# A fused spectral transform and two MLPs in float32 on one core: where GpSimd's background work and six low parts are issued

## The chip, the core and the metric

The kernel runs on one core of a Trainium2 chip. Five engines work side by side: TensorE multiplies matrices (PE in the profile, its weight loads PEld), VectorE (DVE) and ScalarE (ACT) read and write both on-chip memories, GpSimd (POOL) reads and writes SBUF only, and SyncE (SP) issues the DMA transfers. Each engine works through its own instructions strictly in order and waits on semaphores. The metric is the device time of one execution in microseconds (us), as the median of several runs.

## What is computed

The input x is 2 x 3008 x 256 numbers. The reference takes a discrete Fourier transform along both axes, keeps the real part, and sends each of the 6016 tokens through two MLPs of 256 -> 2048 -> 256:

```python
def _attn_ref(x):
    X = np.fft.fft(x, axis=1)
    X = np.fft.fft(X, axis=2)
    return X.real.astype(np.float32)

def _moe_ref(x, w_in, w_out):
    h = x @ w_in
    r = np.maximum(h, 0.0)
    g = r * r
    return (g @ w_out).astype(np.float32)

def _moe2_ref(x, w_in, w_out):
    h = x @ w_in
    g = h * (1.0 / (1.0 + np.exp(-1.702 * h)))
    return (g @ w_out).astype(np.float32)
```

## The kernel before

Every float32 factor is held as a high part (rounded to fp32r) and a low part (the rest), and each product is three matmuls: high by high, high by low, low by high. "Low part" below always means the subtraction that makes such a rest.

The kernel has two halves. The first half transforms x and runs the first MLP; it is a loop of 128 steps, and in the profiled execution it lasts until about 480 us. The second half is the second MLP, in an order written out by hand; the change does not touch it.

A step of the first half takes one block of up to 378 frequency pairs (eight blocks, `blocks`) and one group f of 128 of the 2048 hidden features. Step i consists of:

- `front1` (L462 to L464): six matmuls into one of two `psa` tiles of PSUM. The first three fill its first bank, the other three its second bank.
- VectorE, L805, L807, L808: p from the first bank, then the two halves of h as p plus and minus the second bank. Only after L808 is the `psa` tile free for the front of two `psa` tiles later.
- ScalarE, L814, L815, L817: ReLU, square, and the high part `gh`. In the 14 steps of `SV`, VectorE does ReLU and square in one instruction (L812).
- `low_part` (recorded on L78 as gl<-h,gh): gl = h - gh. It is called for step i in iteration i + 1, behind that iteration's L805 to L808. GpSimd does it, except for the steps in `VSTEPS`, where VectorE does. Only when it has been done is the h buffer free.
- `back` (L477): twelve matmuls of the step four earlier (`LAG`), from its gh and gl, into the block's two accumulators in `psb`.

The h buffers are four (tiles of the tag h, `bufs=4`). Two of them are lent to y from time to time: a block's hidden features are visited in several turns (`turns`), and when a turn ends that isn't the block's first, the partial sums of y that lie in DRAM are fetched into two tiles of the same tag three steps earlier (`ahead`, L589), VectorE adds the accumulators to them (`store`, L602) and SyncE writes them back (L605). This happens in iterations 27, 39, 43 and 51. While the two tiles are lent out, the steps take turns on the other two h buffers: by the addresses of the program, h of step 26 takes the buffer of step 24, h of 27 that of 25, h of 28 that of 26; and from step 38 to 45 h of step k takes that of step k - 2. The accumulators `psb` are both taken by one turn, so the first `back` of the next turn waits for the two additions; it is held back by one step (`held`).

Beside the steps runs background work (`background(i)`, from `PLAN`): widening of weights (`conv` in steps 3 to 36, `w2a` from 58, `w2b` from 88), and the transform of the second batch (`fold3` from step 31, `fold4` from 38, `fold5` from 45, then `even10` and so on). Its instructions go to all engines. GpSimd's share of it from step 18 on is small: the first subtraction of each `fold` (L281), one addition (L207) and some low parts of weights (L78, w and w2i), four sums for each of two weight groups (L234), one low part of eo in each of a few places, and copies of one column (L341, L342).

The code is not issued as traced: a scheduler orders each engine's instructions by when it expects them to be ready, in the order of tracing among those that are ready. From step `THROTTLE` = 18 on, background instructions of VectorE and of ScalarE may not be put ahead of the step's L808 (`last_v`) and L817 (`last_a`); `tc.issue_after(ins)` does that. It fixes the order on that one engine and adds no semaphore wait. GpSimd's background instructions have no such bound.

Steps are counted from 0; the k-th L805 in order of time belongs to step k, and so do the k-th L814 and L817 where no step of `SV` or of the start has been left out. All lines are those of the kernel before.

Of the kernel before, what the change touches and what calls it, by code (L numbers as in the profile page):

```python
# [13 lines left out]
ALU = mybir.AluOpType  # L14
# [27 lines left out]
THROTTLE = 18  # L42

LOW = {(0, 0, 0): "V", (0, 0, 1): "V", (0, 0, 2): "G", (0, 0, 3): "V", (0, 1, 0): "G", (0, 1, 1): "G", (0, 1, 2): "G", (0, 1, 3): "V", (1, 0, 0): "G", (1, 0, 1): "G", (1, 0, 2): "G", (1, 0, 3): "G", (1, 1, 0): "G", (1, 1, 1): "G", (1, 1, 2): "V", (1, 1, 3): "V"}
VSTEPS = {44, 45, 50, 69, 71, 79, 82, 99, 101, 109}
RA = {(0, 0, 0), (0, 0, 1), (0, 0, 2), (0, 0, 3), (0, 1, 1), (0, 1, 2), (0, 1, 3), (1, 0, 1),
      (1, 0, 2), (1, 1, 2), (1, 0, 3), (1, 1, 3)}
EOG = {1, 2, 3}
# [17 lines left out]
def spectral_two_mlps_kernel(  # L66
# [5 lines left out]
    V, A, G, T = nc.vector, nc.scalar, nc.gpsimd, nc.tensor  # L72

    def f32(ap):
        return ap.bitcast(F32)

    def sub(eng, o, a, b):
        eng.tensor_tensor(out=o, in0=a, in1=f32(b), op=ALU.subtract)  # L78
# [19 lines left out]
    def ps_b():  # L98
        return psb.tile([P, 2, 512], F32, tag="b", name="psb")
# [29 lines left out]
    def load_w(mlp, kind, g, slot=None):  # L129
        seen.append((mlp, kind, g))  # L130
        r = raw_tile((len(seen) - 1) % 2 if slot is None else slot)
        nc.sync.dma_start(r, ((w1i, w1o), (w2i, w2o))[mlp][kind][g].bitcast(U32))
        raws[mlp, kind, g] = r
# [134 lines left out]
    def keep_busy(o, k):  # L268

        for _ in range(k):  # L270
            last = T.matmul(o, lhsT=still, rhs=still, start=True, stop=True, skip_group_check=True)
        return last
# [178 lines left out]
    def front1(j, f):  # L451
        wd = WID[blocks[j][1]]
        w = weights[0, 0, f // 4]
        c0 = (f % 4) * P
        t = eo[blocks[j]]
        pq = ps_a()
        if at_step[0] == 0 and j == 0:
            keep_busy(pq[:, 0, 384:512], WARM["first"])
        for par in range(2):
            o = pq[:, par, 0:wd]  # L460
            fs = slice(par * 512 + c0, par * 512 + c0 + P)
            T.matmul(o, lhsT=w[:, 0, fs], rhs=t[:, par, 0, 0:wd], start=True, stop=False)  # L462
            T.matmul(o, lhsT=w[:, 0, fs], rhs=t[:, par, 1, 0:wd], start=False, stop=False)  # L463
            T.matmul(o, lhsT=w[:, 1, fs], rhs=t[:, par, 0, 0:wd], start=False, stop=True)  # L464
        return pq

    def back(j, f, first, last, ecs=range(2)):
        wd = WID[blocks[j][1]]
        if first:
            acc[j] = [ps_b(), ps_b()]  # L470
        gh, gl = gst[j, f]
        w = weights[0, 1, f // 4]
        for ec in ecs:
            e0 = (f % 4) * 256 + ec * P
            for hl, gi in ((0, 0), (0, 1), (1, 0)):
                for s in range(2):
                    T.matmul(  # L477
                        acc[j][ec][:, s, 0:wd],
                        lhsT=w[:, hl, e0:e0 + P],
                        rhs=(gh, gl)[gi][:, s, 0:wd],  # L480
                        start=(first and hl == 0 and gi == 0),
                        stop=(last and hl == 1),
                    )


    def run(gen, n=1 << 30):
        for _ in range(n):
            item = next(gen, None)
            if item is None:
                return False  # L490
            item()
        return True
# [74 lines left out]
    def background(i):  # L567
        for name, rate, job in plan.pop(i, ()):
            live.append((name, rate, job()))
        for entry in list(live):  # L570
            if not run(entry[2], int((i + 1) * entry[1]) - int(i * entry[1])):
                live.remove(entry)
                gone.add(entry[0])
        for name in due.get(i + 1, ()):
            for entry in list(live):
                if entry[0] == name:
                    run(entry[2])
                    live.remove(entry)
                    gone.add(name)
            assert name in gone, name  # L580
# [3 lines left out]
    def ahead(j):  # L584

        wd = WID[blocks[j][1]]
        leaving[j] = [m.tile([P, 2, NP], F32, tag="h", name="o", bufs=4) for _ in range(2)]
        for ec, o in enumerate(leaving[j]):
            nc.sync.dma_start(o[:, :, 0:wd], ydram[j][:, ec, :, 0:wd])  # L589
# [14 lines left out]
                (A.copy, V.tensor_copy)[ec](o, ap)  # L604
            nc.sync.dma_start(y[:, ec, :, 0:wd], o)  # L605

    pend = None
    n = len(steps)


# [162 lines left out]
    for i in range(n):  # L773

        if i == PLAN["fold5"][2]:
            xp.release()
            cv2 = tc.alloc_tile_pool(name="cv2", bufs=1, side="left", reuse_waits="tile")
            w2a = tc.alloc_tile_pool(name="w2a", bufs=3, side="left", reuse_waits="tile")
            load_w(1, *order[0])
            load_w(1, *order[1])  # L780
        if i == PLAN["odd1"][2]:
            cp.release()
            zp.release()
            w2b = tc.alloc_tile_pool(name="w2b", bufs=3, side="left", reuse_waits="tile")
        at_step[0] = i
        if LAG <= i + 1 < n and steps[i + 1 - LAG][4] and steps[i + 1 - LAG][1] in ydram:
            ahead(steps[i + 1 - LAG][1])
        j, f = steps[i][1:3]
        ps = front1(j, f)
        if i == 1:  # L790
            o = ps_b()[:, 0, 0:128]
            for _ in range(WARM["second"]):
                tc.keep_in_program_order(keep_busy(o, 1))
        done = steps[i - LAG][1:] if i >= LAG else None
        if held:
            back(*held.pop())
        if done and done[2] and i > LAG and i < n - 1:
            held.append(done)
        elif done:
            back(*done)  # L800
        wd = WID[blocks[j][1]]
        h = m.tile([P, 2, NP], F32, tag="h", name="h", bufs=4)
        hv = h[:, :, 0:wd]
        p = m.tile([P, NP], F32, tag="p", name="p")
        V.scalar_tensor_tensor(out=p[:, 0:wd], in0=e128[blocks[j]][:, 0:wd], scalar=w1n_t[:, 0, f:f + 1],  # L805
                               in1=ps[:, 0, 0:wd], op0=ALU.mult, op1=ALU.add)
        V.tensor_tensor(out=h[:, 0, 0:wd], in0=p[:, 0:wd], in1=ps[:, 1, 0:wd], op=ALU.add)  # L807
        last_v = V.tensor_tensor(out=h[:, 1, 0:wd], in0=p[:, 0:wd], in1=ps[:, 1, 0:wd], op=ALU.subtract)  # L808
        if done and done[3]:
            store(*done[:2])  # L810
        if i in SV:
            V.scalar_tensor_tensor(out=hv, in0=hv, scalar=0.0, in1=hv, op0=ALU.max, op1=ALU.mult)  # L812
        else:
            A.activation(out=hv, in_=hv, func=AF.Relu)  # L814
            A.activation(out=hv, in_=hv, func=AF.Square)  # L815
        gh = mg.tile([P, 2, NP], F32R, tag="gh", name="gh", bufs=5)
        last_a = A.copy(gh[:, :, 0:wd], hv)  # L817

        def low_part(i, key, h, gh):
            pw = WID[blocks[key[0]][1]]  # L820
            gl = mg.tile([P, 2, NP], F32R, tag="gl", name="gl", bufs=5)
            sub(G if i not in VSTEPS else V, gl[:, :, 0:pw], h[:, :, 0:pw], gh[:, :, 0:pw])
            gst[key] = (gh, gl)

        if pend:
            low_part(*pend)
        pend = (i, (j, f), h, gh)
        with ExitStack() as behind:
            if THROTTLE <= i < n:
                behind.enter_context(tc.issue_after(last_v.ins))  # L830
                behind.enter_context(tc.issue_after(last_a.ins))
            background(i)
    low_part(*pend)
    assert not live
    np_.release()
# [45 lines left out]
    with tc.manual_schedule():  # L881
        for u in range(units + 2):
# [3 lines left out]
            pw = WID2[(u - 1) // 8] if 0 < u <= units else 0  # L886
# [24 lines left out]
            if u > 0 and u <= units:  # L911
                gh = (m3, m2)[(u - 1) % 2 == 0].tile([P, 4, NP2], F32R, tag="gh", name="gh")[:, :, 0:pw]
# [35 lines left out]
            if u > 0 and u <= units:  # L948
                gl = m3.tile([P, 4, NP2], F32R, tag="gl", name="gl", bufs=2)[:, :, 0:pw]
# [144 lines left out]
```

## Time and profile before

| | |
|---|---|
| median of 3 runs | 980.89 us (980.37 to 982.03) |
| the profiled execution, its own time | 979.26 us |
| its span, first to last instruction | 977.5 us |
| TensorE busy (matmuls) | 956.6 us, 98% |
| VectorE busy | 696.9 us, 71% |
| ScalarE busy | 599.9 us, 61% |
| GpSimd busy | 327.1 us, 33% |
| mean granted TensorE clock | 0.996 |

How to read it: the profile comes from one execution. Busy time is the time in which an engine had an instruction in work. Matmuls overlap each other, so that what counts for TensorE is the idle time and the distance from one matmul's start to the next. A row of the order of time gives start, duration, engine, line, what is written and read, and in brackets the engine's idle time just before and what ended it. PEclk is the granted share of TensorE's full clock.

### The profile page before, as it was taken

To read this page: it belongs to the slowest core of one execution; us is meant where nothing else is said; L and a number is where in the kernel's file an instruction comes from. 1 tells how busy PE (TensorE), PEld (TensorE's weight loads), DVE (VectorE), ACT (ScalarE), POOL (GpSimd) and SP (SyncE) were. 2 spreads that over 40 slices of the span, in tenths; PEclk is the share of its full clock that TensorE was granted. 3 is DMA by queue.
4 is the path that set the end of the run, shared out by engine and by line. 5 is a ranking of instruction groups with operands and counts; after the bars stand their busy time and mean duration, and the time that the engine had idled before them with its cause. 6 is when DMAs were issued, how large, how long until landed. Compare 5 with 4: busy or idle time off the path is not lost.

```text
span 977.5 us, 12510 instructions
## 1 busy us (share of the span) xinstructions
PE 956.6 (98%) x4872; PEld 855.4 (88%) x4872; DVE 696.9 (71%) x870; ACT 599.9 (61%) x700; POOL 327.1 (33%) x203
## 2 busy tenths in 40 slices
PE   9899989999999999999999999999999999999997
PEld 9579979998999799999978888888888888888996
DVE  7996788986889778896688865566566466556653
ACT  3588878665776578768876654454455455445442
POOL 5357667643575457656412220020002002000000
PEclk9999999999999999999999999999999999999999
DMA  7641232411021001010131020011011002000001
GB/s 302 219 147 53 75 111 98 128 59 56 1 76 44 17 17 44 32 44 33 44 118 44 1 86 1 1 46 41 1 44 43 1 1 81 1 1 5 39 1 39
DMA packets 21899, 53.58 MB, mean 55 GB/s; under 512 B 3280, under 2 KB 15184, under 8 KB 19152
## 3 DMA queue, kind: packets, MB, share of 16 engines
q1 hardware_dynamic: 21840, 52.79, 15.5%
q8 instruction: 38, 0.62, 0.3%
q14 instruction: 21, 0.17, 0.1%
HBM read 37.36 MB, written 15.42 MB: 54 GB/s over the span
## 4 chain that ended last, share of the span: by engine, by line
PE 79%; DVE 11%; ACT 5%; issue 3%; POOL 2%; DMA 0%; DVEq 0%; ACTq 0%; POOLq 0%
PE psb L872 26%; PE psc L856 22%; PE psb L477 20%; PE psa L462 3%; PE psa L464 3%; PE psa L463 3%; PE psa L361 2%; ACT h L814 1%; ACT h L815 1%; DVE p L805 1%; DVE h L808 1%; DVE h L807 1%; ACT gh L817 1%; DVE ue L185 1%; DVE ue L638 1%
## 5 line engine op out<-in xcount | busy, mean ns | idle before, releaser
L78 POOL TENSOR_TENSOR gl<-h,gh 128x752 fp32r<-128x752 f32 (+1 forms) x118 | 220.3, 1872 | 158.4 <-ACT gh L817 128.4
L477 PE MATMUL psb<-gh,w 128*128 128x376 f32 (+1 forms) x1024 | 239.0, 336 | 1.1 <-DVE o L604 0.9
L477 PEld LDWEIGHTS psb<-gh,w 128*128 128x128 f32 x1024 | 183.5, 189 | 1.9 <-issue 1.2
L872 PE MATMUL psb<-gh,w 128*128 128x512 f32 (+1 forms) x576 | 163.7, 386 | 0.0
L936 DVE TENSOR_TENSOR g<-u,psc 128x1024 f32<-128x1024 f32 (+1 forms) x48 | 57.6, 1199 | 115.5 <-PE psc L856 115.5
L814 ACT ACTIVATE h<-h 128x752 f32<-128x752 f32 (+1 forms) x114 | 94.8, 833 | 62.2 <-DVE h L808 58.9
L477 PE MATMUL psb<-gl,w 128*128 128x376 f32 (+1 forms) x512 | 130.8, 336 | 0.0
L938 ACT ACTIVATE g<-g 128x1536 f32<-128x1536 f32 (+1 forms) x48 | 70.4, 1467 | 95.0 <-DVE g L936 95.0
L872 PEld LDWEIGHTS psb<-gh,w 128*128 128x128 f32 x576 | 108.1, 188 | 20.6
L817 ACT CAST gh<-h 128x752 fp32r<-128x752 f32 (+1 forms) x128 | 105.0, 822 | 31.8 <-DVE h L812 24.9
L78 DVE TENSOR_TENSOR gl<-g,gh 128x2048 fp32r<-128x2048 f32 (+1 forms) x48 | 109.2, 2275 | 1.2 <-ACT gh L913 1.2
L638 POOL TENSOR_TENSOR ue<-raw 128x512 f32<-128x512 f32 (+1 forms) x10 | 22.2, 2240 | 254.4 <-DMA raw<-ydram 248.1
L805 DVE SCALAR_TENSOR_TENSOR p<-n,w1n_t,psa 128x376 f32<-128x376 f32 (+1 forms) x128 | 76.5, 600 | 43.1 <-PE psa L464 42.8
L815 ACT ACTIVATE h<-h 128x752 f32<-128x752 f32 (+1 forms) x114 | 95.1, 835 | 3.1
L462 PE MATMUL psa<-eo,w 128*128 128x376 f32 (+1 forms) x256 | 88.2, 345 | 7.3 <-DVE h L808 5.1
L477 PEld LDWEIGHTS psb<-gl,w 128*128 128x128 f32 x512 | 93.3, 190 | 0.0
L913 ACT CAST gh<-g 128x2048 fp32r<-128x2048 f32 (+1 forms) x48 | 90.2, 1879 | 0.1
L872 PE MATMUL psb<-gl,w 128*128 128x512 f32 (+1 forms) x288 | 87.7, 386 | 0.0
L463 PE MATMUL psa<-eo,w 128*128 128x376 f32 (+1 forms) x256 | 85.8, 335 | 0.0
L464 PE MATMUL psa<-eo,w 128*128 128x376 f32 (+1 forms) x256 | 85.6, 334 | 0.0
L807 DVE TENSOR_TENSOR h<-p,psa 128x376 f32<-128x376 f32 (+1 forms) x128 | 69.8, 545 | 20.6 <-POOL gl L78 7.6
L935 ACT ACTIVATE g<-psc 128x512 f32<-128x512 f32 (+1 forms) x48 | 28.4, 591 | 76.1 <-PE psc L856 76.1
(151 smaller groups left out, 1548.7 us busy)
## 6 DMA issues: line engine op xcount, KB each, us to landing
ydram<-o SPq DMA_DIRECT2D x17, 376.0 KB, 3.0
xt<-in_x SPq DMA_DIRECT2D x5, 1024.0 KB, 6.8
out<-o SPq DMA_DIRECT2D x10, 512.0 KB, 2.6
cst<-in_dfts SPq DMA_DIRECT2D x8, 570.0 KB, 5.9
raw<-in_w1i SPq DMA_DIRECT2D x4, 1024.0 KB, 4.9
raw<-in_w1o SPq DMA_DIRECT2D x4, 1024.0 KB, 6.4
raw<-in_w2i SPq DMA_DIRECT2D x4, 1024.0 KB, 4.8
raw<-in_w2o SPq DMA_DIRECT2D x4, 1024.0 KB, 4.9
```

What stands on the lines that cost most here:

```text
L78: eng.tensor_tensor(out=o, in0=a, in1=f32(b), op=ALU.subtract)
L462: T.matmul(o, lhsT=w[:, 0, fs], rhs=t[:, par, 0, 0:wd], start=True, stop=False)
L463: T.matmul(o, lhsT=w[:, 0, fs], rhs=t[:, par, 1, 0:wd], start=False, stop=False)
L464: T.matmul(o, lhsT=w[:, 1, fs], rhs=t[:, par, 0, 0:wd], start=False, stop=True)
L477: T.matmul(acc[j][ec][:, s, 0:wd], lhsT=w[:, hl, e0:e0 + P], rhs=(gh, gl)[gi][:, s, 0:wd], start=(first and hl == 0 and gi == 0), stop=(la ...
L805: V.scalar_tensor_tensor(out=p[:, 0:wd], in0=e128[blocks[j]][:, 0:wd], scalar=w1n_t[:, 0, f:f + 1], in1=ps[:, 0, 0:wd], op0=ALU.mult, op1= ...
L814: A.activation(out=hv, in_=hv, func=AF.Relu)
L815: A.activation(out=hv, in_=hv, func=AF.Square)
L817: last_a = A.copy(gh[:, :, 0:wd], hv)
L856: T.matmul(bank, lhsT=w[:, hl, slot * P:(slot + 1) * P], rhs=x[:, yl, 0:wd], start=(first and hl == 0 and yl == 0), stop=(hl == 1), skip_g ...
L872: T.matmul(o[:, s, 0:wd], lhsT=w[:, hl, e0:e0 + P], rhs=g[:, 2 * i + s, 0:wd], start=(f == 0 and hl == 0 and g is gh), stop=(f == 15 and h ...
L913: A.copy(gh, gs[u - 1])
```

## The change

There are two parts. First, `low_part` returns its instruction where GpSimd makes it, the loop keeps the latest one as `last_g`, and from step 18 on GpSimd's background instructions of an iteration are ordered behind `last_g`. Since `low_part` for step i - 1 is called just ahead of `background(i)`, that is the low part of step i - 1, or the latest before it that GpSimd made. Second, steps 25, 26, 37, 38, 41 and 42 join `VSTEPS`: VectorE makes their low parts. These are the two steps ahead of each of the additions in iterations 27, 39 and 43.

```diff
-VSTEPS = {44, 45, 50, 69, 71, 79, 82, 99, 101, 109}
+VSTEPS = {25, 26, 37, 38, 41, 42, 44, 45, 50, 69, 71, 79, 82, 99, 101, 109}
@@
-    pend = None
+    pend = last_g = None
@@
-            sub(G if i not in VSTEPS else V, gl[:, :, 0:pw], h[:, :, 0:pw], gh[:, :, 0:pw])
+            low = G if i not in VSTEPS else V
+            last = low.tensor_tensor(out=gl[:, :, 0:pw], in0=h[:, :, 0:pw], in1=f32(gh[:, :, 0:pw]), op=ALU.subtract)
             gst[key] = (gh, gl)
-
-        if pend:
-            low_part(*pend)
+            return last if low is G else None
+
+        last_g = (low_part(*pend) if pend else None) or last_g
         pend = (i, (j, f), h, gh)
         with ExitStack() as behind:
             if THROTTLE <= i < n:
                 behind.enter_context(tc.issue_after(last_v.ins))
                 behind.enter_context(tc.issue_after(last_a.ins))
+                if last_g is not None:
+                    behind.enter_context(tc.issue_after(last_g.ins))
             background(i)
```

## Rows read from the trace of the kernel before

**Rows 1.** The page: busy time, share of span, instructions per engine.
```profile
PE 956.6 (98%) x4872; PEld 855.4 (88%) x4872; DVE 696.9 (71%) x870; ACT 599.9 (61%) x700; POOL 327.1 (33%) x203
```

**Rows 2.** Busy time by stretch; columns: stretch, length, engines, clock, DMA share, GB/s.
```profile
127.00:144.00 17.00, 12.87 (x62) 11.59 (x61) 12.12 (x21) 13.07 (x16) 13.07 (x7) 0.90 0.28 95
144.00:168.00 24.00, 24.00 (x140) 24.00 (x139) 21.57 (x34) 20.73 (x26) 16.57 (x9) 1.00 0.26 88
168.00:196.00 28.00, 26.39 (x160) 25.88 (x159) 25.11 (x37) 20.41 (x27) 18.13 (x12) 1.00 0.43 132
196.00:300.00 104.00, 104.00 (x613) 101.16 (x612) 81.61 (x128) 69.55 (x90) 55.28 (x38) 1.00 0.13 43
```

**Rows 3.** TensorE in order of time: front of step 29, then first back of step 24.
```profile
139.18 0.44 PE L462 MATMUL psa<-eo,w 128*128 128x378 f32 x1 [3.47 <-DVE h L808]
...
140.12 0.97 PE L477 MATMUL psb<-gh,w 128*128 128x378 f32 x2 [0.16 <-ACT h L814]
```

**Rows 4.** VectorE in order of time: h of steps 26 and 27, then y's additions.
```profile
133.79 0.54 DVE L808 TENSOR_TENSOR h<-p,psa 128x378 f32<-128x378 f32 x1
...
138.12 0.55 DVE L807 TENSOR_TENSOR h<-p,psa 128x378 f32<-128x378 f32 x1 [3.27 <-POOL gl L78]
138.58 0.54 DVE L808 TENSOR_TENSOR h<-p,psa 128x378 f32<-128x378 f32 x1
139.04 1.78 DVE L602 TENSOR_TENSOR o<-o,psb 128x752 f32<-128x752 f32 x2
```

**Rows 5.** GpSimd in order of time, steps 25 to 27 and fold3's subtraction.
```profile
133.95 2.39 POOL L281 TENSOR_TENSOR t<-xt 128x1024 f32<-128x1024 f32 x1 [1.80 <-DVE w L78]
136.29 3.55 POOL L78 TENSOR_TENSOR gl<-h,gh 128x756 fp32r<-128x756 f32 x2
```

**Rows 6.** ScalarE in order of time: gh of steps 25 and 26, then background work.
```profile
132.78 0.83 ACT L817 CAST gh<-h 128x756 fp32r<-128x756 f32 x1
...
136.16 0.82 ACT L817 CAST gh<-h 128x756 fp32r<-128x756 f32 x1
...
137.91 1.12 ACT L174 ACTIVATE ue<-raw 128x1024 uint32<-128x1024 uint32 x1
```

**Rows 7.** VectorE's ten low parts of before: durations in ns, min/median/max.
```profile
L78 DVE TENSOR_TENSOR gl<-h,gh x10: 933/1310/1761, 200.1 to 426.0; 128x752 fp32r<-128x752 f32 x7, 128x756 fp32r<-128x756 f32 x3
```

**Rows 8.** VectorE in order of time: fold3's L299, then steps 37 to 44.
```profile
161.99 0.42 DVE L299 TENSOR_TENSOR xt<-xt 128x256 f32<-128x256 f32 x1
...
168.49 0.61 DVE L805 SCALAR_TENSOR_TENSOR p<-n,w1n_t,psa 128x376 f32<-128x376 f32 x1 [1.38 <-PE psa L464]
...
185.39 2.59 DVE L299 TENSOR_TENSOR xt<-xt 128x256 f32<-128x256 f32 x1
...
189.68 0.55 DVE L807 TENSOR_TENSOR h<-p,psa 128x376 f32<-128x376 f32 x1 [1.18 <-POOL gl L78]
...
190.59 1.10 DVE L300 TENSOR_TENSOR xt<-xt 128x256 f32<-128x256 f32 x1
...
194.96 0.60 DVE L805 SCALAR_TENSOR_TENSOR p<-n,w1n_t,psa 128x376 f32<-128x376 f32 x1
```

**Rows 9.** GpSimd in order of time: steps 37 and 38, and fold5's subtraction.
```profile
173.06 1.82 POOL L78 TENSOR_TENSOR gl<-h,gh 128x752 fp32r<-128x752 f32 x1 [1.08 <-ACT gh L817]
177.89 1.84 POOL L78 TENSOR_TENSOR gl<-h,gh 128x752 fp32r<-128x752 f32 x1 [3.00 <-DVE h L808]
...
185.29 2.41 POOL L281 TENSOR_TENSOR t<-xt 128x1024 f32<-128x1024 f32 x1 [2.00 <-DMA xt<-in_x]
```

**Rows 10.** TensorE in order of time: the front of step 45.
```profile
195.62 0.44 PE L462 MATMUL psa<-eo,w 128*128 128x376 f32 x1 [1.47 <-DVE p L805]
```

**Rows 11.** Order of time: GpSimd's low parts of steps 30 and 31; VectorE's second addition of fold3.
```profile
155.17 4.08 POOL L78 TENSOR_TENSOR gl<-h,gh 128x756 fp32r<-128x756 f32 x2 [2.72 <-ACT gh L817]
156.84 0.70 DVE L288 TENSOR_TENSOR xt<-t 128x512 f32<-128x512 f32 x1
```

**Rows 12.** GpSimd's sums for w2's first group, in order of time.
```profile
271.40 3.20 POOL L234 TENSOR_TENSOR ue<-ue 128x256 f32<-128x256 f32 x4 [1.16 <-DVE ue L187]
```

## The prediction, made before the change was timed

> **What bounds the kernel now.** I read the page first: TensorE is busy 98% of the span, VectorE 71%, GpSimd 33% [rows 1]. So time can only be won where TensorE idles or runs at a lower clock, and those places are few. The stretches of the loop show them [rows 2]: from 127 to 144 us TensorE is busy 12.87 of 17.00 us and its granted clock is 0.90; from 144 to 168 it is never idle; from 168 to 196 it is busy 26.39 of 28.00; from 196 to 300 never idle. What the change touches lies in steps 18 to 46, that is between about 102 and 200 us, and nearly all of what can be won there is 4.13 us + 1.61 us of idle time, and the clock: 10% of 17 us, 1.7 us. Together 7.4 us, 0.76% of the time.
>
> Then I followed the two gaps back. **First gap:** the front of step 29 waits 3.47 us for L808 of step 27 [rows 3]. That L808 is late since VectorE stood 3.27 us before L807, waiting for GpSimd's low part of step 25 [rows 4], whose h buffer step 27 takes (two of the four are lent to y). GpSimd could have made it earlier: ScalarE had gh of step 25 at 132.78 + 0.83 = 133.61 [rows 6]. But the first subtraction of fold3 stood ahead in GpSimd's queue: it waited 1.80 us for VectorE to leave its tile and ran from 133.95 to 136.34; then came the low parts of steps 25 and 26 in one go, to 139.84 [rows 5]. Fold3 belongs to step 31; the scheduler had put it five steps ahead. Behind the front comes a small second wait, 0.16 us, until 140.12: the first back of the new turn needs the accumulators, which VectorE's additions at 139.04 free [rows 3, 4]. **Second gap:** the front of step 45 waits 1.47 us for p of step 44 [rows 10]. Here VectorE itself is the limit: it is in step with TensorE at 168.49 (it waited 1.38 us for TensorE) and then works to 194.96, when p of step 44 begins, with 25.11 us busy of the 28 us of the stretch [rows 8, 2]. From 168.49 to 194.96 are 26.47 us, and the gap of 1.47 says that 25.0 would have been in time.
>
> **The change part by part.** *GpSimd's order.* No semaphore is added; what is new is who stands in front of whom on GpSimd. Fold3's subtraction moves from ahead of the low part of step 25 to behind that of step 30. Fold5's, which ran 185.29 to 187.70 [rows 9] ahead of the low part of step 40, moves behind step 43's, and that low part no longer waits for it. Fold4's subtraction and one addition of the weights (L207) move by a few steps, with work for which nothing stood still. The sums for w2 (four in 3.20 us at 271.40) are spread over the low parts of four steps [rows 12]; TensorE does not idle from 196 to 300 us [rows 2], so I cost that at nothing; if that cover were gone, it would cost at most those 3.20 us. The rest of GpSimd's background work already stands behind a low part of its own step.
>
> *First gap with both parts.* L808 of step 26 ends at 133.79 + 0.54 = 134.33 [rows 4], gh of step 25 is there, and VectorE makes the low part in 0.93 us at best [rows 7], to 135.3. Then p (0.60 us) and h of step 27: 0.60 + 0.46 + 0.54 = 1.6 us from starts and durations like those of [rows 4, 8], so L808 of step 27 ends near 136.9 and not at 139.12. The front of step 29 goes on 2.2 us earlier. Next late is the accumulator: the low part of step 26 now stands on VectorE ahead of the two additions. Its gh ends at 136.16 + 0.82 = 136.98 [rows 6], it takes to 137.9, and the first addition (half of 1.78 us [rows 4]) to 138.8. The first back starts at 138.9 where it started at 140.12 [rows 3]: 1.2 us gained. TensorE then stands twice, some 1.2 and 1.5 us, and no more for 3.5 in one piece; if its clock stays up, the 1.7 us come back too. Sum for this place: 1.2 + 1.7 = **2.9 us**. It can't be much more: VectorE idled 17.00 - 12.12 = 4.9 us of the stretch [rows 2], and two low parts of 0.93 take 1.9 of them; so it gets ahead by 3.0 us at most, and ScalarE has background work until 137.91 + 1.12 = 139.03 [rows 6] whatever VectorE does, unless the scheduler moves that. Lower bound: 1.2 us (clock falls all the same). Upper bound: all of the 5.8 us of this stretch, if the new order of VectorE and ScalarE is smoother than the old one.
>
> *Second gap.* The low parts of steps 37 and 38 were not late on GpSimd: it began them without a queue, after idling 1.08 and 3.00 us [rows 9], and the steps that take their buffers did not wait. VectorE gets them and those of 41 and 42, in the one stretch where it is the limit. Four at 0.93 are 3.7 us; at 1.31, the median of its ten [rows 7], 5.2 us. I take 4.5: GpSimd has less to do then, but is not idle. Against that stand the wait for the low part of step 40, 1.18 us; L299, which took 2.59 us beside fold5's subtraction and 0.42 otherwise [rows 8], and now meets a low part of 1.82 [rows 9] in place of 2.41: 0.6; and L300, 1.10 in place of 0.42: 0.7. Together 2.5 us. So p of step 44 comes 4.5 - 2.5 = **2.0 us** later against TensorE than before, with bounds from 1.2 less the luck of other meetings, say 0, to 4.
>
> That meeting is a thing to look at. L299 began at 185.39, a moment behind fold5's subtraction, and ended at 187.98, 0.28 us after that one ended at 187.70 [rows 8, 9]; alone it takes 0.42. It did not run slower, it stood. The Trainium skill says why (SBUF — State Buffer, "SBUF: two separate sides"): VectorE with two SBUF inputs and GpSimd share a port pair that is an exclusive lock, and who comes second waits for the whole instruction of the other. By that rule a low part moved to VectorE costs 0.93 us only where GpSimd is idle. The trace agrees with it here.
>
> *Other queues.* VectorE's additions in iterations 39 and 43 come 0.9 us later by one low part each, and with them SyncE's stores of y. Nothing in these stretches waits for those stores longer than VectorE waits for itself; I cost them at nothing and, uncovered, at 0.9 us each. ScalarE's order may shift in any way; no cost, no row for it.
>
> **Sum.** 2.9 gained, 2.0 given back at step 45: 0.9 us. The profiled execution took 979.26 us, so it would be 978.4. The median is 980.89, 1.63 us above that execution; I carry the difference over: 980.89 - 0.9 = **980.0 us**. A tenth of a percent is less than the 0.2% (1.96 us) that a measurement of this kernel can tell from no change.
>
> **The rivals.** *VectorE is the new bound at step 45 (slower).* What the first gap gives is lost, since VectorE can't keep up in steps 37 to 44: its four low parts each meet a GpSimd instruction. At 1.76 us, the longest of the ten [rows 7], they cost 7.0, less 2.5: the gap of 1.47 us grows by 4.5 to 6.0. A gap of 3.47 us was followed by a lower clock that cost 1.7 us, one of 1.47 was not (the clock is 1.00 from 168 to 300 [rows 2]); so this one would be followed by it. 1.2 to 2.9 gained, 4.5 + 1.7 lost: 3.3 to 5.0 slower, 984 to 986 us; it decides against the change as soon as the low parts cost 1.2 us each and the clock falls. For it: VectorE's 25.11 of 28 us. Against: it has fewer meetings, as GpSimd loses four of its low parts there. 24%, mostly at its near end, 983.
>
> *Both gaps close (faster).* The scheduler orders everything anew, and if VectorE's other background work falls into its 4.9 us of idle time in the first stretch, TensorE idles there hardly at all: up to 5.8 us. If, at step 45, the low parts cost 0.93 and meet nothing, only 1.2 is given back. 4.6 us: 976.3; with half of that, 978.6. For it: every single wait of the first gap is one that the change takes away. Against: y's additions follow one more low part. 36%.
>
> *Fold3 too late.* Its subtraction (2.39 us) behind the low part of step 30, which ended near 155.17 + 1.82 = 157.0 [rows 11], ends at 159.4; VectorE's second addition of fold3 reads it and stood at 156.84 [rows 11], in order. So VectorE waits 2.6 us, with all of step 33 behind it. TensorE did not idle there [rows 2], so that some is covered; what comes through is 0 to 2 us: 980 to 982. It is part of "no change".
>
> *The order hardly alters anything,* since most of GpSimd's work stood right already: 980.9, part of "no change" too.
>
> **How the numbers follow.** No change that can be told, 40%, with the forecast of 980.0 us and its own range from 979.0 to 982.8; faster 36%; slower 24%. The range for 8 in 10: below, it reaches to the faster rival with both of its terms, 976.0; above, to the near end of the slower one, 983.5.
>
> **What would show it.** Right: GpSimd's order of time has fold3's subtraction behind step 30's low part; VectorE's wait before L807 of step 27 is gone; the gap before step 29 is under 1.5 us, and PEclk from 127 to 150 us is 1.00; the gap before the front of step 45 is 2.5 to 4.5 us. Wrong: if that last gap is no larger than 1.47, VectorE had room that I did not see, and the time is near 977; if a new wait stands at L288, or the clock falls in either stretch, it is above 981.

## The result, and the profile after

| | before | after |
|---|---|---|
| median | 981.04 us of 7 runs on the same chip | 986.68 us of 7 runs (985.99 to 991.76) |
| the profiled execution, its own time | 979.26 us | 985.99 us |
| its span | 977.5 us | 984.2 us |

The ratio of after to before is 1.0064, with an interval of 1.0048 to 1.0081: the change makes the kernel slower by about 5.6 us. The forecast was 980.0 us and its range ended at 983.5.

The page of after, engines as in [rows 1]: TensorE's busy time rises only by 2.4 us, VectorE's by 11.7, and GpSimd's falls by 9.0.

```profile
span 984.2 us, 12499 instructions
...
PE 959.0 (97%) x4872; PEld 856.9 (87%) x4872; DVE 708.6 (72%) x876; ACT 598.9 (61%) x700; POOL 318.1 (32%) x197
```

The stretches of [rows 2], with the same columns, of after:

```profile
127.00:144.00 17.00, 14.66 (x73) 13.68 (x72) 15.70 (x24) 13.94 (x17) 7.16 (x4) 0.90 0.34 120
144.00:168.00 24.00, 20.83 (x118) 19.89 (x116) 22.35 (x24) 13.94 (x18) 14.64 (x8) 1.00 0.25 88
168.00:196.00 28.00, 24.75 (x135) 23.91 (x136) 24.91 (x39) 18.52 (x25) 11.22 (x7) 0.94 0.33 107
196.00:300.00 104.00, 102.92 (x608) 99.73 (x607) 82.00 (x131) 72.42 (x94) 54.90 (x36) 1.00 0.15 50
```

The stretch from 144 to 168 us, in which TensorE was never idle before, now has 3.17 us of idle time, and the clock falls in the one behind it.

To place the loss I took, for every step, the start of its first L462 in the one trace less that in the other. After stands behind before by 1.02 us at step 29, -1.01 at step 30 (the first gap got 2.03 us shorter), 0.02 at step 32, 0.02 at step 35, **5.36 at step 37**, 5.70 at step 39, 7.94 at step 46 and 6.7 at the end. The 1.02 us at the start are there from step 18 on, ahead of all that the change touches; every kernel below has 0.9 to 2.5 us of it; the profiled execution of before was 1.63 us under its median. So nearly the whole loss, 5.34 us, comes in two steps for which I had no cost in the sum.

TensorE in order of time, at the ends of its longer waits in after up to step 37 (start, duration, line, what is written and read; in brackets the idle time before and what ended it):

```profile
138.55 0.44 PE L462 MATMUL psa<-eo,w 128*128 128x378 f32 x1 [1.82 <-DVE h L808]
...
149.46 0.44 PE L462 MATMUL psa<-eo,w 128*128 128x378 f32 x1 [0.78 <-DVE h L808]
...
166.01 0.44 PE L462 MATMUL psa<-eo,w 128*128 128x376 f32 x1 [1.19 <-DVE p L805]
169.22 0.44 PE L462 MATMUL psa<-eo,w 128*128 128x376 f32 x1 [2.42 <-DVE h L808]
```

Behind the first of these and behind the last two the granted clock is low; two stretches by themselves, columns as above:

```profile
139.00:144.00 5.00, 5.00 (x21) 5.00 (x21) 5.00 (x8) 4.60 (x7) 1.30 (x1) 0.66 0.33 120
...
170.00:174.00 4.00, 4.00 (x17) 4.00 (x16) 2.88 (x7) 3.87 (x6) 1.81 (x1) 0.57 0.00 0
```

So the front of step 36 waits 1.19 us ahead of its first half and 2.42 ahead of its second, 3.61 us, and behind it TensorE runs for a while at the lower of its two clocks (1.2 GHz): a mean of 0.57 over 4.00 us costs 0.43 x 4.00 = 1.7 us. 5.3 us together. Both waits are for VectorE. VectorE and GpSimd in order of time at that place, in after (L823 is the line that makes the low parts there; in before it is the helper's L78):

```profile
160.89 2.32 DVE L287 TENSOR_TENSOR xt<-t 128x512 f32<-128x512 f32 x1 [1.38 <-POOL t L281]
163.14 2.30 DVE L288 TENSOR_TENSOR xt<-t 128x512 f32<-128x512 f32 x1
165.36 0.59 DVE L805 SCALAR_TENSOR_TENSOR p<-n,w1n_t,psa 128x378 f32<-128x378 f32 x1
165.88 1.76 DVE L293 TENSOR_TENSOR xt<-xt 128x512 f32<-128x512 f32 x1
167.57 0.68 DVE L298 TENSOR_TENSOR xt<-xt 128x512 f32<-128x512 f32 x1
```

```profile
156.66 1.83 POOL L823 TENSOR_TENSOR gl<-h,gh 128x756 fp32r<-128x756 f32 x1 [2.68 <-ACT gh L817]
158.44 2.42 POOL L281 TENSOR_TENSOR t<-xt 128x1024 f32<-128x1024 f32 x1
160.82 6.28 POOL L823 TENSOR_TENSOR gl<-h,gh 128x756 fp32r<-128x756 f32 x3
```

Fold3's subtraction (L281) runs right behind the low part of step 30, as the change orders it. VectorE's addition L287 overwrites what L281 reads, so VectorE stands 1.38 us for it. The scheduler has moved L287 as well: it now stands behind L808 of step 33, and in before it ran ahead of p of step 32:

```profile
154.59 0.68 DVE L287 TENSOR_TENSOR xt<-t 128x512 f32<-128x512 f32 x1
```

Then comes what I had not seen: L281 has held up the low part of step 31, whose gh was done at 157.31, and that one those of steps 32 and 33 (gh done at 161.15 and 162.75). The three now run as a train, 160.82 to 167.10, just while VectorE goes through the rest of fold3. L287, L288 and L293 take 2.32, 2.30 and 1.76 us, where each of the three takes 0.68 when nothing stands in its way (as L298 does here, behind the train; L288 of before took 0.70 [rows 11]). They wait for the train, one car each. That is 1.64 + 1.62 + 1.08 + 1.38 = 5.7 us of VectorE; 2.1 of it is covered, the rest reaches TensorE.

### The profile page after: what moved, and what is told of

The parts are those of the page before. It is cut to its first block, busy times and chain, and to the rows that moved or that the text cites. A ratio compares the mean times of both kernels' runs of the same rounds, so it can differ in the third digit from the quotient of the medians.

```text
span 984.2 us, 12499 instructions
## 1 busy us (share of the span) xinstructions
PE 959.0 (97%) x4872; PEld 856.9 (87%) x4872; DVE 708.6 (72%) x876; ACT 598.9 (61%) x700; POOL 318.1 (32%) x197
## 4 chain that ended last, share of the span: by engine, by line
PE 62%; DVE 4%; ACT 2%; issue 1%; DVEq 0%; ACTq 0%
PE psb L875 26%; PE psc L859 22%; PE psb L477 9%; PE psa L462 1%; PE psa L464 1%; PE psa L463 1%; ACT gh L817 0%; DVE h L807 0%; DVE p L805 0%; ACT h L815 0%; ACT h L814 0%; DVE ue L185 0%; DVE h L808 0%; PE psa L361 0%; DVE h L812 0%
## 5 line engine op out<-in xcount | busy, mean ns | idle before, releaser
L823 POOL TENSOR_TENSOR gl<-h,gh 128x752 fp32r<-128x752 f32 (+1 forms) x112 | 210.0, 1878 | 183.6 <-ACT gh L817 158.2
L78 DVE TENSOR_TENSOR gl<-g,gh 128x2048 fp32r<-128x2048 f32 (+1 forms) x48 | 108.8, 2266 | 1.2 <-ACT gh L916 1.2
L462 PE MATMUL psa<-eo,w 128*128 128x376 f32 (+1 forms) x256 | 88.2, 345 | 9.1 <-DVE h L808 6.3
L807 DVE TENSOR_TENSOR h<-p,psa 128x376 f32<-128x376 f32 (+1 forms) x128 | 69.7, 545 | 16.8 <-POOL gl L823 5.3
```

The lines of the kernel that those rows point to most:

```text
L823: last = low.tensor_tensor(out=gl[:, :, 0:pw], in0=h[:, :, 0:pw], in1=f32(gh[:, :, 0:pw]), op=ALU.subtract)
```

## The experiments

**Theories.** At first two: A, fold3's subtraction comes too late and VectorE waits for it; B, the four low parts that VectorE gets in steps 37 to 42 are the loss. Neither fitted the first four runs, and a third took their place: C, *port meetings*: each instruction of VectorE with two inputs in SBUF that comes upon a running instruction of GpSimd stands until that one ends, so it matters how much of GpSimd's work lies beside VectorE's background work and how many pieces come in a row. All times are medians. "Front 30 to 38" and the like is the change of the shift against before, as worked out above.

**Part 1 alone** (`VSTEPS` as before).

> The first part alone: GpSimd's background work behind the low part from step 18 on, VSTEPS as before. Theory A (fold3 too late): fold3's subtraction stands behind step 30's low part here too, VectorE's additions of fold3 meet it and the low parts behind it one after the other, and TensorE stands around step 36 as in the changed kernel; the first gap shrinks by about 2 us, the second by 1 (fold5's subtraction is out of the way). So 3 to 5 us slower than the kernel before, 984 to 986 us. Theory B (VectorE's four low parts of steps 37 to 42 are the cost): these are on GpSimd here, so it is 1 to 3 us faster than before, 978 to 980 us.

```diff
-VSTEPS = {25, 26, 37, 38, 41, 42, 44, 45, 50, 69, 71, 79, 82, 99, 101, 109}
+VSTEPS = {44, 45, 50, 69, 71, 79, 82, 99, 101, 109}
```

Measured: 983.79 us, ratio 1.0028 (1.0017 to 1.0038). The first gap gains 4.05 us, twice as much as with both parts, and steps 30 to 38 lose 6.5. VectorE at fold3 in this kernel:

```profile
159.84 2.30 DVE L287 TENSOR_TENSOR xt<-t 128x512 f32<-128x512 f32 x1 [1.88 <-POOL t L281]
162.07 2.26 DVE L288 TENSOR_TENSOR xt<-t 128x512 f32<-128x512 f32 x1
```

So part 1 brings both the gain and the new loss; that speaks for A (the time is just under its range), but the two additions are too long as well. And the second gap brings nothing: steps 38 to 46 lose 1.1 us, where A had a gain of 1.

**Part 2 alone** (before with the changed `VSTEPS`).

> The second part alone: six low parts on VectorE, GpSimd's background work free as before, so that fold3's subtraction stands early. Theory A: no stall around step 36; the low part of step 25 on VectorE meets fold3's subtraction (until 136.3 us) and gains only 1 us at the first gap; steps 37 to 45 give back 2. So 0 to 2 us slower than before, 981 to 983 us. Theory B: the four low parts bring most of the 5.6 us that the whole change lost: 984 to 986 us.

```diff
-VSTEPS = {44, 45, 50, 69, 71, 79, 82, 99, 101, 109}
+VSTEPS = {25, 26, 37, 38, 41, 42, 44, 45, 50, 69, 71, 79, 82, 99, 101, 109}
```

Measured: 987.17 us, ratio 1.0074 (1.0056 to 1.0091). A is missed: here nothing is held behind a low part, and front 30 to 38 still loses 4.4 us. B has nearly the number, but not the place: steps 38 to 46 lose 1.7.

**The whole change without iteration 31's binding**, so that fold3's subtraction stands where the scheduler puts it.

> The whole change, but GpSimd's background work of iteration 31 alone (fold3's subtraction) is left free, as before. Theory A: the 5.7 us lost between steps 30 and 37 are gone; what is left is a first gap of 2 us and 2 us given back at steps 39 to 45: 980 to 982 us. Theory B: nearly as slow as the whole change, 985 to 987 us.

```diff
-                if last_g is not None:
+                if last_g is not None and i != 31:
```

Measured: 983.27 us, ratio 1.0031 (1.0017 to 1.0045). That lies between A and B. Front 30 to 38 loses nothing at all, as A has it, but the first gap gains only 0.6; steps 38 to 46 lose 3.7. The profiled execution was the longest of its eight (987.76 us); the 4.3 us that it loses behind step 60 are in none of these numbers.

**Low parts of steps 25 and 26 on VectorE, nothing else.**

> The kernel before with steps 25 and 26 alone added to VSTEPS. Both theories: the first gap (3.47 us) shrinks to 1 to 2 us; if VectorE stays in step afterwards, 1 to 3 us faster than before, 978 to 980 us. If low parts on VectorE are costly wherever they stand (theory B in its strict form), the gain is eaten up by fold3's work behind it: 981 us or more.

```diff
-VSTEPS = {44, 45, 50, 69, 71, 79, 82, 99, 101, 109}
+VSTEPS = {25, 26, 44, 45, 50, 69, 71, 79, 82, 99, 101, 109}
```

Measured: 986.6 us, ratio 1.0053 (1.0041 to 1.0065), far from the 978 to 980 us of both theories; only the strict form of B (981 us or more) had the sign. Front 30 to 38 loses 4.0 us. VectorE and GpSimd in this kernel, at the first gap and at fold3 (the L281 at 162.45 is fold4's):

```profile
136.67 2.37 DVE L78 TENSOR_TENSOR gl<-h,gh 128x756 fp32r<-128x756 f32 x1
...
159.71 2.16 DVE L288 TENSOR_TENSOR xt<-t 128x512 f32<-128x512 f32 x1
...
162.71 2.70 DVE L293 TENSOR_TENSOR xt<-xt 128x512 f32<-128x512 f32 x1
165.34 2.28 DVE L298 TENSOR_TENSOR xt<-xt 128x512 f32<-128x512 f32 x1
```

```profile
135.85 2.38 POOL L281 TENSOR_TENSOR t<-xt 128x1024 f32<-128x1024 f32 x1 [1.80 <-DVE w L78]
...
157.68 3.64 POOL L78 TENSOR_TENSOR gl<-h,gh 128x756 fp32r<-128x756 f32 x2 [2.67 <-ACT gh L817]
162.45 2.42 POOL L281 TENSOR_TENSOR t<-xt 128x1024 f32<-128x1024 f32 x1 [1.13 <-DMA xt<-in_x]
164.82 4.45 POOL L78 TENSOR_TENSOR gl<-h,gh 128x756 fp32r<-128x756 f32 x2
```

The low part that VectorE took over costs 2.37 us, not 0.93: it runs into the very subtraction of fold3 that it was to get around. And some 20 us later, at fold3, L288, L293 and L298 meet three of GpSimd's instructions in turn, with no wait on a semaphore anywhere. This is where theory C comes from. The Trainium skill has the rule (SBUF — State Buffer, "SBUF: two separate sides"): the port pair that VectorE and GpSimd share is a lock for a whole instruction, and the one that comes second is blocked. The trace agrees in both directions: L288 here stands 1.48 us, while [rows 11] show L288 in 0.70 us beside two low parts that took 4.08 us instead of 3.66.

**Part 1 with fold3's subtraction behind the low part of step 28** instead of 30. (The text below calls L281 fold3's second subtraction; fold3 has one, on GpSimd.)

> GpSimd's background work stands behind the low parts as in the changed kernel, all low parts are on the engines that had them before, and the second subtraction of fold3 (iteration 31) alone is held two low parts less: behind that of step 28. Theory 'port meetings and the wait for fold3': in the run with this first part alone (983.79 us) the step from 29 to 30 gained 4.1 us and steps 35 to 37 lost 5.5 us, behind a wait of 1.88 us for fold3's subtraction. If that wait is the cause, the gain stays and the loss goes: 977 to 979 us against 981.0 before. Theory 'held work costs wherever it is held': the loss moves to steps 31 to 34 and stays in size: 983 to 984 us. Theory 'GpSimd's order is worth nothing by itself': 981 us.

```diff
+        if i == 29:
+            g_28 = last_g
...
-                    behind.enter_context(tc.issue_after(last_g.ins))
+                    behind.enter_context(tc.issue_after((g_28 if i == 31 else last_g).ins))
```

Measured: 978.66 us, ratio 0.9974 (0.9966 to 0.9983): faster than before. The first gap gains 4.07 us and front 30 to 38 loses 1.07. GpSimd and VectorE there:

```profile
149.54 2.42 POOL L281 TENSOR_TENSOR t<-xt 128x1024 f32<-128x1024 f32 x1
151.91 1.85 POOL L823 TENSOR_TENSOR gl<-h,gh 128x756 fp32r<-128x756 f32 x1
156.13 4.38 POOL L823 TENSOR_TENSOR gl<-h,gh 128x756 fp32r<-128x756 f32 x2 [2.37 <-ACT gh L817]
```

```profile
155.91 0.68 DVE L287 TENSOR_TENSOR xt<-t 128x512 f32<-128x512 f32 x1
...
158.13 0.69 DVE L288 TENSOR_TENSOR xt<-t 128x512 f32<-128x512 f32 x1
```

GpSimd is through with fold3 before VectorE comes, and no train stands behind it: it idles 2.37 us. The additions take 0.68 and 0.69; where they meet the two later low parts, it is those that stand (4.38 us for 3.66). Steps 38 to 46 lose 3.2 us in this profiled execution, the longest of the twelve at 980.83 us. 1.7 of them are one more fall of the clock, behind a wait of 1.50 us at 196.86 (a mean of 0.76 from 196 to 203 us). The others have less of that: nine of them have a mean clock of 0.997 or 0.998, this one 0.995.

**The same behind step 29.**

> The first part alone with fold3's second subtraction behind the low part of step 29: half way between the run with step 30 (983.8 us) and that with step 28 (978.7 us). Theory 'there is an edge': the second addition L287 of fold3 needs the subtraction to be done by the time VectorE comes to it; behind step 29 the subtraction ends some 2 us earlier than behind step 30, where VectorE waited 1.88 us for it, so nothing is left of the wait, the clock stays up and the time is 978 to 980 us. Theory 'each step of holding costs the same': 981 to 982 us.

```diff
-        if i == 29:
+        if i == 30:
```

Measured: 981.96 us, ratio 1.0014 (1.0005 to 1.0023). My "edge" is missed. No semaphore wait is left, and front 30 to 38 loses as much as behind step 30, 6.75 us. Half of that, 3.4 us, is one stretch of low clock, a mean of 0.57 from 158 to 166 us, twice as long as the others; steps 38 to 46 then give 1.5 us back. VectorE and GpSimd:

```profile
150.40 2.46 DVE L283 TENSOR_TENSOR t<-xt 128x1024 f32<-128x1024 f32 x1
152.79 3.43 DVE L78 TENSOR_TENSOR w<-ue,w 128x1024 fp32r<-128x1024 f32 x1
156.15 2.26 DVE L287 TENSOR_TENSOR xt<-t 128x512 f32<-128x512 f32 x1
```

```profile
149.94 1.85 POOL L823 TENSOR_TENSOR gl<-h,gh 128x756 fp32r<-128x756 f32 x1 [1.97 <-ACT gh L817]
151.75 3.39 POOL L281 TENSOR_TENSOR t<-xt 128x1024 f32<-128x1024 f32 x1
155.10 4.98 POOL L823 TENSOR_TENSOR gl<-h,gh 128x756 fp32r<-128x756 f32 x2
```

The two engines take turns: L283 stands for the low part (L283's shortest is 1.21 us), L281 stands for L283 (3.39 for 2.42), VectorE's w stands for L281 (3.43 for 1.21), the next low part stands for w, L287 stands for that low part. 1.2 + 2.2 + 1.6 = 5.0 us of VectorE, without any dependency between the two. This run parts A from C: VectorE is late with no wait for fold3.

**The whole change, GpSimd's low parts of steps 27 to 36 in two halves each.**

> The changed kernel whole, with GpSimd's low parts of steps 27 to 36 made in two instructions of half the size each. Theory 'port meetings': an instruction of VectorE that meets one of GpSimd's stands until that one ends; with halves it stands at most 0.9 us instead of 1.8, so the time that VectorE's instructions take above their shortest falls from 6.3 to about 3 us in steps 30 to 38, the clock does not fall there, and the time is 982 to 984 us. Theory 'wait for fold3 alone': only the 1.4 us that VectorE stands for fold3's subtraction matter, the halves change nothing in that: 986 to 987 us. Against both: each half has a start of its own on GpSimd, and if those cost 0.2 us each, nothing is won.

```diff
-            last = low.tensor_tensor(out=gl[:, :, 0:pw], in0=h[:, :, 0:pw], in1=f32(gh[:, :, 0:pw]), op=ALU.subtract)
+            for r in (slice(0, 1), slice(1, 2)) if low is G and 27 <= i <= 36 else (slice(0, 2),):
+                last = low.tensor_tensor(out=gl[:, r, 0:pw], in0=h[:, r, 0:pw], in1=f32(gh[:, r, 0:pw]), op=ALU.subtract)
```

Measured: 983.8 us, ratio 1.0028 (1.0016 to 1.0039), 2.9 us less than the change whole. VectorE waits for fold3's subtraction as before, 1.51 us, but what follows is shorter:

```profile
159.74 1.49 DVE L287 TENSOR_TENSOR xt<-t 128x512 f32<-128x512 f32 x1 [1.51 <-POOL t L281]
161.16 1.50 DVE L288 TENSOR_TENSOR xt<-t 128x512 f32<-128x512 f32 x1
...
163.09 0.97 DVE L293 TENSOR_TENSOR xt<-xt 128x512 f32<-128x512 f32 x1
163.99 1.47 DVE L298 TENSOR_TENSOR xt<-xt 128x512 f32<-128x512 f32 x1
```

A stand of 1.6 us becomes one of 0.8, TensorE's wait before step 37 is 1.93 us, and the clock stays up there: 3.4 us lost from front 30 to 38 in place of 6.7. That is C's range; but the time above the shortest fell from 6.3 to 4.7 us and not to about 3, and steps 38 to 46 lose 4.3.

**Before with the low parts of steps 37, 38, 41 and 42 on VectorE.**

> The kernel before with the low parts of steps 37, 38, 41 and 42 on VectorE and nothing else. It measures the prediction's second term by itself: four low parts for 4.5 us less 2.5 us of waits that they remove, 2.0 us later at step 45: 983 us. Theory 'port meetings': each of the four meets an instruction of GpSimd or not; with one meeting in two they cost 5.5 us, and the time is 983 to 985 us. Theory 'VectorE has room there' (the changed kernel without the wait for fold3 lost 3.7 us in steps 38 to 46, with another order of TensorE's work): no more than 1 us: 981 to 982 us.

```diff
-VSTEPS = {44, 45, 50, 69, 71, 79, 82, 99, 101, 109}
+VSTEPS = {37, 38, 41, 42, 44, 45, 50, 69, 71, 79, 82, 99, 101, 109}
```

Measured: 982.23 us, ratio 1.0019 (1.0006 to 1.0032). Front 38 to 46 loses 0.85 us: my second term by itself is about 1 us, not 2.0. By the median it is 1.1, just outside the 981 to 982 us of "VectorE has room there"; "port meetings" had 2 us or more.

**Before with all of GpSimd's low parts from step 18 on in halves** (the same edit as above, `i >= 18`, without the binding).

> The kernel before with each of GpSimd's low parts from step 18 on made in two instructions of half the size, order otherwise as before. Theory 'port meetings': VectorE's stand behind a low part falls from at most 1.8 us to at most 0.9; the first gap (3.47 us) is made by a subtraction of fold3 and stays; of the 3.4, 2.2 and 3.3 us that VectorE's instructions take above their shortest in the three stretches of eight steps from 23 to 46 up to half goes: 979 to 981 us. Rival 'the start of an instruction costs more than the meeting': GpSimd's low parts become longer by 0.1 to 0.3 us each, the low parts come later, 982 to 984 us.

Measured: 980.81 us, ratio 0.9998 (0.9990 to 1.0007): no difference. In this kernel, where TensorE loses nothing at fold3, shorter pieces bring nothing.

**The whole change, with fold3 behind step 28.**

> The changed kernel whole, with fold3's second subtraction held behind the low part of step 28 and not of step 30. It asks whether the two parts add up: holding it there took the first part alone from 983.8 to 978.7 us, 5.1 us. Theory 'the wait for fold3 is the whole loss of steps 33 to 36': the same 5 us here, 986.7 less 5 = 981.5 to 982.5 us; what then stays above the first part alone (about 3 us) is what the second part costs, partly in steps 38 to 46. Theory 'the second part does no harm once fold3 is early': 978 to 980 us.

The edit is the one of part 1 above, on the changed kernel. Measured: 982.48 us, ratio 1.0015 (1.0006 to 1.0023), 4.2 us less than the change whole. Front 30 to 38 loses 1.07, as in part 1 with step 28; the rest, 3.8 us more than that kernel, is part 2: the first gap gains 2.04 and not 4.07, and steps 38 to 46 lose 3.9, where part 1 with step 28 loses 3.2, or 1.5 without the clock's fall in its profiled execution.

**Part 1 with fold3 behind step 28, binding only up to iteration 37.**

> The first part alone with fold3's second subtraction behind the low part of step 28, and the binding ended at iteration 37, so that fold4's and fold5's work and the sums for w2 stand as before from there on. In the run with the binding to the end, the front of step 46 came 3.2 us later against that of step 38 than before. Theory 'that is the price of the binding in steps 38 to 46': it comes back in part, 976 to 978 us. Theory 'the binding is worth nothing or little there': the same 978.7 us.

```diff
-                if last_g is not None:
+                if last_g is not None and i < 38:
```

Measured: 979.68 us, ratio 0.9982 (0.9973 to 0.9991). No gain over 978.66, as the second theory has it: the binding behind step 37 costs nothing in sum. Steps 38 to 46 lose 1.8 us here.

**Part 1 with fold3 behind step 28, and all low parts of GpSimd from step 18 on in halves.**

> The first part alone with fold3's second subtraction behind the low part of step 28, and GpSimd's low parts from step 18 on in two instructions of half the size. By themselves the halves changed nothing that can be told (ratio 0.9998), as the time that VectorE stood longer stayed where it was. Theory 'port meetings matter only where VectorE is late': 978 to 979.5 us, no gain over the same without halves. Theory 'shorter meetings help in steps 38 to 46, where 5.2 us of VectorE's time are above its shortest': 976.5 to 978 us.

The two edits are those above. Measured: 977.02 us (975.99 to 978.09, five executions), ratio 0.9959 (0.9946 to 0.9971): the fastest of all, 4.1 us under before. Steps 38 to 46 lose only 0.7 us. GpSimd is busier, 370.6 us against 327.1 [rows 1]: 100 low parts of 1.82 us in the median have become pairs of 1.00 each, which is 18 us more, and the rest is halves that took longer than that. Yet TensorE is busy all of the 104 us from 196 to 300. The interval overlaps that of the kernel with whole low parts, so that the halves' own share (1.6 us by the medians) is less certain than the gain over before. This is the version that I would keep.

What VectorE stood, and what came of it, in the eight steps around fold3. The first column is worked out from all of VectorE's instructions between p of step 30 and p of step 38: the duration of each less the shortest of its kind and shape in these eight steps of any kernel.

| kernel | above the shortest, us | front 30 to 38 loses, us |
|---|---|---|
| before | 2.2 | 0 |
| part 1, fold3 behind step 28 | 2.1 | 1.1 |
| before, steps 37, 38, 41 and 42 on VectorE | 2.7 | 0.0 |
| part 1, fold3 behind step 28, bound up to 37 | 3.0 | 1.1 |
| before, GpSimd's low parts in halves | 3.0 | 0.0 |
| part 1, fold3 behind step 28, halves | 3.3 | 1.0 |
| whole change, iteration 31 not bound | 4.0 | 0.0 |
| whole change, fold3 behind step 28 | 4.2 | 1.1 |
| whole change, halves in steps 27 to 36 | 4.7 | 3.4 |
| part 1 | 4.8 | 6.5 |
| part 1, fold3 behind step 29 | 5.5 | 6.8 |
| whole change | 6.3 | 6.7 |
| part 2 | 6.8 | 4.4 |
| before, steps 25 and 26 on VectorE | 7.1 | 4.0 |

Up to 4.2 us TensorE loses at most 1.1 (in all but part 1 with halves that is a wait in step 31, ahead of fold3); from 4.7 on it falls behind, and mostly the clock falls with it. The order within the lower half isn't that of the stands, since the waits for L281 and the falls of the clock come on top.

## Why the prediction was wrong

**What failed: the cost of holding fold3's subtraction, which stands in the prediction as the rival "Fold3 too late" and in the sum at nothing.** Its mechanism was right as far as it went, and I named the sign to look for, a new wait at L288 (it stands one line earlier, at L287). Its size was not: 0 to 2 us were to come through, and 5.34 did, 3.61 as waits of TensorE and 1.7 by the clock. I costed the semaphore wait, 2.6 us, and it was 1.38, since VectorE did steps 32 and 33 first. I did not cost what the held subtraction does to the queue behind it, namely that the next three low parts run as a train beside VectorE's fold3, and each instruction that meets a car of it stands 1.1 to 1.6 us; nor the 1.7 us of clock behind the wait. All the pieces lay in [rows 8, 9]: I had seen L299 stand for fold5's subtraction, drew the rule from it, and used it for the moved low parts alone. So a term of its own was left in "no change". (The range's upper end, 983.5, also lay below the 984 at which my slower rival began.)

**First gap.** Expected: 1.2 + 1.7 = 2.9 us gained. Measured: 2.03. The wait before L807 of step 27 is gone, as said, and the front of step 29 still waits 1.82 us. Here is why, VectorE in after:

```profile
134.81 0.54 DVE L808 TENSOR_TENSOR h<-p,psa 128x378 f32<-128x378 f32 x1
135.27 0.60 DVE L805 SCALAR_TENSOR_TENSOR p<-n,w1n_t,psa 128x378 f32<-128x378 f32 x1
135.79 0.94 DVE L823 TENSOR_TENSOR gl<-h,gh 128x756 fp32r<-128x756 f32 x1
136.65 0.93 DVE L602 TENSOR_TENSOR o<-o,psb 128x752 f32<-128x752 f32 x1
137.49 0.54 DVE L807 TENSOR_TENSOR h<-p,psa 128x378 f32<-128x378 f32 x1
137.95 0.55 DVE L808 TENSOR_TENSOR h<-p,psa 128x378 f32<-128x378 f32 x1
```

The low part of step 25 takes its 0.94 us, as forecast, but y's first addition slips between it and h of step 27, and L808 ends at 138.5. The forecast was 136.9, which is 137.9 in the time of after (1.02 us behind here). The waits give more than the 1.2 us all the same: TensorE's idle time from 127 to 144 us is 2.34 us in place of 4.13. What does not come is the term of 1.7 us: the clock falls behind the wait that is left, 0.90 in both stretches. With the low parts left on GpSimd the gap is 0.96 us (part 1 alone) and the clock stays up, 1.00 from 127 to 144 us: part 1 is the whole of that gain, and part 2 takes half of it back. My working had it the other way round, with the low parts on VectorE as the remedy. (That L281 waited 1.80 us in before "for VectorE to leave its tile" is not in the row: it names VectorE's low part of w, which L281 neither reads nor writes. What it waited for stays open.) And a wait of 0.78 us in step 31, which I had not foreseen, takes 1.03 back at once; all the kernels above that hold fold3 lose 0.8 to 1.1 us there, but the last.

**Second gap.** Expected: 2.0 us given back, as 4.5 for four low parts less 2.5. After gives back 2.24 from step 39 to 46, and the four cost 1.95 + 0.93 + 0.94 + 0.94 = 4.8 us. The size is right, the place is not: there is no longer gap before step 45, but three of 0.91, 0.92 and 1.05 us at 185.14, 189.43 and 203.20. And the four low parts alone lose 0.85 us, and part 1 alone, which was to take waits away here, loses 1.1: together nearly the 2.24, but from other terms, so that the agreement is luck. With fold3 behind step 28 both parts lose 3.9, and without iteration 31's binding 3.7; what takes the 1.5 to 2 us more stays open. TensorE's own order changes there too when both parts are in, and no run parts that from the low parts.

**The rest.** Moving w2's sums cost nothing, as forecast: TensorE is 102.92 of 104 us busy from 196 on, and 1.05 of the rest is the wait at 203.20. That moving fold5's subtraction gains is not shown: with the binding ended at iteration 37 steps 38 to 46 lose 1.8 us, and with it 1.5 without the clock's fall. The rival "VectorE is the new bound at step 45" had the sign and, at 984 to 986 us, nearly the time, but it put the loss some nine steps later than it came.

## What to carry to other kernels

When an instruction of GpSimd is held back, look at what is queued behind it and which of VectorE's SBUF work it will then run beside: the train, not the wait, was most of the price for VectorE here (4.3 of 5.7 us), and 0.68 us became 2.3. Hold each piece of background work by when its reader comes, not all by one rule: behind step 28 the held subtraction made the kernel 2.5 us faster, behind 29 it was 0.8 slower, behind 30 2.8. A low part moved to VectorE to get around GpSimd costs GpSimd's time all the same if it meets what it should avoid (2.37 us for 0.93).

## What was not expected of the hardware

The two engines can lock into turns. In the kernel with fold3 behind step 29 they met with both queues full, and from then on each next instruction of one stood for that of the other, though none depends on it; GpSimd's 2.42 us became 3.39 and VectorE's 1.21 became 3.43.

The clock does not fall by the length of the last wait alone. The wait of 1.82 us before step 29 in after is followed by a mean granted clock of 0.66 from 139 to 144 us; one of 1.83 us at the same front, in the whole change with halves in steps 27 to 36, by 1.00:

```profile
139.04 0.44 PE L462 MATMUL psa<-eo,w 128*128 128x378 f32 x1 [1.83 <-DVE h L808]
```

```profile
139.00:144.00 5.00, 4.96 (x28) 4.96 (x29) 5.00 (x8) 4.62 (x6) 0.83 (x1) 1.00 0.42 154
```

That kernel's later waits of 1.93 and 1.99 us, at 166.43 and 182.80, were not followed by a fall either. And a wait of 1.50 us at 196.86 was followed by one (part 1 with fold3 behind step 28), while one of 1.50 at 201.16 in part 1 alone was not, nor that of 1.47 [rows 10]. So the 1.7 us that such a fall mostly costs can't be put down to a wait of this size with certainty, nor left out.
